# Fused linear attention and MLP on one core: batch 2's loads lose a wait, the first unit's transposes and exps are reordered, and the planner gets new offsets

## The chip, the cores and the metric

One core of one Trainium2 chip. The metric is the device time of one execution in microseconds (us): lower is better. The engines of the core are TensorE (PE, matrix products and transposes), VectorE (DVE), ScalarE (ACT), GpSimd (POOL) and SyncE (SP, which here only issues transfers). PE's weight loads have a row of their own in the profile (PEld).

## The reference

```python
def phi(x):
    proj = np.einsum('bhsd,df->bhsf', x, w_phi)
    proj = proj - np.max(np.abs(proj), axis=-1, keepdims=True)
    return np.concatenate([np.exp(proj), np.exp(-proj)], axis=-1)
q_p, k_p = (phi(q), phi(k))                       # 8 batches x 8 heads x 576 x 256
kv = np.einsum('bhsf,bhsd->bhfd', k_p, v)
z = np.sum(k_p, axis=2)
num = np.einsum('bhsf,bhfd->bhsd', q_p, kv)
den = np.einsum('bhsf,bhf->bhs', q_p, z)[..., None] + 1e-06
x = (num / den), heads side by side               # 8 x 576 x 512
...
mu = np.mean(x, axis=-1, keepdims=True)
var = np.mean((x - mu) ** 2, axis=-1, keepdims=True)
xn = (x - mu) / np.sqrt(var + 1e-06) * g_ln
ch = np.maximum(xn @ w_ch1, 0.0) @ w_ch2          # 512 -> 2048 -> 512
return (x + ch).astype(np.float32)
```

q, k and v are 8 x 8 x 576 x 64 in float32; the profile counts 36.77 MB read and 9.44 MB written.

## The kernel before, in words

**Units.** The attention is cut into 32 units of two heads each, eight to a pair of batches (NPAIR = 4, H = 8). In the first two pairs (STAGED = 2) units 0 to 3 are four pairs of heads of one batch and units 4 to 7 those of the next; in the last two pairs unit i is head i of both batches. So batch 0 is units 0 to 3, batch 1 units 4 to 7, **batch 2 units 8 to 11**, batch 3 units 12 to 15. The 576 rows of a head are 512 main rows and a tail of 64; the tails of two heads share one mixed tile.

**A unit's stages.** Its q, k and v are loaded (`load_main`, `load_tails`, both through `issue`, L544, nearly all on SP) into three rotating buffers for two units each (qk0 to qk2, v0 to v2; tails in qx and vx). Units 0 to 7 are transposed on PE (`a_trans`: main tiles L688, the mixed tile L696, with copies out of PSUM on DVE or ACT); later units are cast to bf16 (L754, L759 on DVE, L761 on ACT, L763 on POOL, into three buffers b16) and transposed by a DMA (L782). The products with w_phi go into PSUM (k and q L876 or L882, tails L891, mixed tile L804/L805). DVE takes the maxima (L944), ACT the exps: exp(+k) and exp(-k) L958, the tails' L1024, the mixed tile's L821/L826/L830, and the factors em (L949) and en (L963) from the maxima, with which POOL scales v (vv, L968, L973, L977). PE forms kv (L1050, L1056), the result is copied as KV (L1064 on DVE, L1066 on ACT), PE forms the numerator (L1120, L1128, L1134), and the quotient is put into x (L1164, L1172, L1183, L1189); the part that lies on the other half of the partitions goes by way of xs and is moved by a transfer on SP (`x_158<-xs_132`, L1081).

**The MLP.** A pair of batches that is through gets its statistics (L1317), is centred (L1337 on DVE, L1342, L1347) and transposed: the first pair on PE with copies that apply g (L1278, L1288 on DVE, L1290 on ACT), the others by DMA (L1303). Then follow the products with w_ch1 (L1396), the relu into hT_all (L1405 on DVE, L1407 on ACT), the products with w_ch2 (L1465), the result with the residual (L1473 on DVE, L1478 on ACT with L1484 on POOL), and the store. The weights are loaded in four parts each on POOL's queue, converted on the way: w_ch1 by `load_w1` (L636), each part once the unit named in GATE has come; w_ch2 by `load_w2` (L647).

**What sets the order.** Nothing is ordered by hand: each operation is entered into a planner (class `Order`, L153) with its engine or engines, an estimate of its duration, what it reads and writes and a rank. `run` (L204) plays the program through and gives each engine, whenever it comes free, the ready operation of the lowest rank; that order is what is emitted. An operation's rank is the latest time at which it may start for the rest to be in time, plus an offset from the table OFF, chosen by the unit (`stage_table`, L1536) and the stage. One number can so move many instructions. Each engine then runs its list strictly in order and waits where an operand is missing. Where the planner sees PE idle before WARM = 75 us, it puts a filler into PE's order (`fill`, L1676): a product of zeros, `wz`, of 120 columns.

**The hold.** A load that is entered with `hold=True` waits for the fourth part of w_ch2 (`wait_for_w2`, L559, HOLD = 3), on the chip as in the plan. In the kernel before these are the loads of units 8 to 15, that is of batches 2 and 3. The load stands in SP's order, so all that SP issues behind it waits too.

## Time and profile before

| what | value |
|---|---|
| runs | 376.31, 374.83, 377.27 us; median 376.31 |
| profiled execution | 375.71 us, of which 373.9 us in the span |
| granted clock of PE | 1.0 |
| products with w_ch1 (L1396) and w_ch2 (L1465) | 152.5 and 139.2 us of PE's time |
| DVE maxima (L944) | 77.2 us |
| ACT exps of k (L958) and of the tails (L1024) | 61.0 and 60.2 us |
| transfers | 53.39 MB, 143 GB/s in the mean |

The span is the time from the profile's first to its last instruction. Busy times of engines overlap; a group is named by its line, engine, operation and out<-in with buffer numbers left out. A row of the waits reads: the waiting engine and what it wanted to run, an arrow, what came last, then total, number and longest wait. The chain of work that ended last gives start, length and what ran. "SPq" is SP as the issuer of transfers, "DMA" the transfer itself.

### The profile page before, as it was taken

To read this page: it belongs to the slowest core of one execution; us is meant where nothing else is said; L and a number is where in the kernel's file an instruction comes from. 1 tells how busy PE (TensorE), PEld (TensorE's weight loads), DVE (VectorE), ACT (ScalarE), POOL (GpSimd) and SP (SyncE) were. 2 spreads that over 40 slices of the span, in tenths; PEclk is the share of its full clock that TensorE was granted. 3 is DMA by queue.
4 is the path that set the end of the run, shared out by engine and by line. 5 is a ranking of instruction groups with operands and counts; after the bars stand their busy time and mean duration, and the time that the engine had idled before them with its cause. 6 is when DMAs were issued, how large, how long until landed. Compare 5 with 4: busy or idle time off the path is not lost.

```text
span 373.9 us, 9770 instructions
## 1 busy us (share of the span) xinstructions
PE 361.6 (97%) x3732; PEld 229.5 (61%) x3776; DVE 246.3 (66%) x548; ACT 269.5 (72%) x586; POOL 203.6 (54%) x340
## 2 busy tenths in 40 slices
PE   8999999999899999999999999999999999999996
PEld 8889865556556655556566755655656555555544
DVE  4679998869779998988867899758786900000001
ACT  2888987786959996986978797787775845444430
POOL 4539757798575669956767608367456321011112
PEclk9999999999999999999999999999999999999999
DMA  8999979999997776686751539330000361010012
GB/s 205 285 236 268 193 204 253 224 244 234 300 191 186 209 180 203 145 219 127 233 136 33 132 100 168 93 65 29 31 30 30 86 127 46 12 56 28 31 56 84
DMA packets 91438, 53.39 MB, mean 143 GB/s; under 512 B 57840, under 2 KB 86832, under 8 KB 91392
## 3 DMA queue, kind: packets, MB, share of 16 engines
q1 hardware_dynamic: 86352, 47.73, 52.1%
q0 software_dynamic: 4416, 4.49, 7.3%
q10 hardware_dynamic: 624, 0.56, 0.6%
q8 instruction: 29, 0.48, 0.5%
q14 instruction: 17, 0.14, 0.1%
HBM read 36.77 MB, written 9.44 MB: 124 GB/s over the span
## 4 chain that ended last, share of the span: by engine, by line
PE 82%; DMA 5%; DVE 5%; ACT 4%; issue 1%; SPq 1%; POOL 0%; DVEq 0%; ACTq 0%
PE b_bank L1396 31%; PE b_bank L1465 30%; PE n_bank L1677 4%; PE a_bank L882 3%; PE n_bank L1056 3%; DMA qk<-in_q_dram 3%; PE a_bank L1128 2%; PE a_bank L891 2%; DVE m L944 2%; DMA qkT<-b 2%; PE n_bank L1050 1%; ACT ea L1024 1%; PE b_bank L1430 1%; PE n_bank L1128 1%; ACT eb L958 1%
## 5 line engine op out<-in xcount | busy, mean ns | idle before, releaser
L1396 PE MATMUL b_bank<-xT,w 128*128 128x384 bf16 (+2 forms) x768 | 152.5, 326 | 0.8 <-ACT hT_all L1407 0.3
L1465 PE MATMUL b_bank<-w,hT_all 128*128 128x512 bf16 x519 | 139.2, 379 | 2.0 <-issue 0.2
L1396 PEld LDWEIGHTS <-w 128*128 128x128 bf16 x768 | 70.9, 98 | 54.8 <-issue 2.2
L1407 ACT ACTIVATE hT_all<-b_bank 128x384 bf16<-128x384 f32 (+2 forms) x126 | 61.9, 492 | 53.8 <-PE b_bank L1396 53.0
L944 DVE TENSOR_REDUCE m<-a_bank 128x8 f32<-128x1024 f32 x64 | 77.2, 1215 | 16.3 <-PE a_bank L882 13.2
L1465 PEld LDWEIGHTS <-hT_all 128*128 128x128 bf16 x560 | 51.0, 98 | 42.3 <-issue 1.3
L1484 POOL TENSOR_TENSOR o<-o,x 128x512 f32<-128x512 f32 x22 | 25.4, 1156 | 70.6 <-ACT o L1478 65.5
L958 ACT ACTIVATE eb<-a_bank 128x1024 bf16<-128x1024 f32 x60 | 61.0, 1045 | 3.8 <-DVE m L944 3.7
L1024 ACT ACTIVATE ea<-a_bank 128x1024 bf16<-128x1024 f32 x60 | 60.2, 1040 | 2.7 <-PE a_bank L891 1.0
L968 POOL TENSOR_TENSOR vv<-v,em 128x512 bf16<-128x512 f32 x30 | 31.4, 1048 | 34.4 <-ACT em L949 23.2
L1172 POOL TENSOR_TENSOR x<-numc,rden 128x192 bf16<-128x192 f32 (+2 forms) x44 | 25.0, 572 | 38.2 <-DVE rden L1164 37.3
L1405 DVE TENSOR_SCALAR hT_all<-b_bank 128x384 bf16<-128x384 f32 (+2 forms) x66 | 36.7, 558 | 9.2 <-PE b_bank L1396 8.5
L1473 DVE SCALAR_TENSOR_TENSOR o<-b_bank,rstd,x 128x512 f32<-128x512 f32 x13 | 9.7, 744 | 47.3 <-issue 25.9
L968 POOL TENSOR_TENSOR vv<-v,en 128x512 bf16<-128x512 f32 x30 | 31.4, 1047 | 2.0 <-ACT en L963 1.9
L1677 PE MATMUL n_bank<-wz 128*128 128x120 bf16 x389 | 29.1, 228 | 0.0
L1128 PEld LDWEIGHTS <-ea 128*128 128x128 bf16 x448 | 22.0, 97 | 9.1 <-issue 2.1
L1677 PEld LDWEIGHTS <-wz 128*128 128x128 bf16 x411 | 25.9, 105 | 1.0 <-issue 0.3
L1056 PE MATMUL n_bank<-vv,eb 128*128 128x65 bf16 x480 | 25.2, 194 | 0.0
L1317 DVE BATCH_NORM_STATS2 st<-x 128x6 f32<-128x256 bf16 (+1 forms) x52 | 25.0, 506 | 0.1
L1056 PEld LDWEIGHTS <-eb 128*128 128x128 bf16 x480 | 20.9, 98 | 3.5
L1478 ACT ACTIVATE o<-b_bank,rstd 128x512 f32<-128x512 f32 x22 | 15.1, 686 | 10.0 <-PE b_bank L1465 9.7
L882 PE MATMUL a_bank<-wbk,qkT 64*128 64x128 bf16 x448 | 19.7, 217 | 0.3 <-DMA qkT<-b 0.3
(132 smaller groups left out, 509.4 us busy)
## 6 DMA issues: line engine op xcount, KB each, us to landing
out_dram<-o SPq DMA_DIRECT2D x31, 256.0 KB, 2.5
qk<-in_k_dram SPq DMA_DIRECT2D x24, 256.0 KB, 4.8
qk<-in_q_dram SPq DMA_DIRECT2D x23, 256.0 KB, 5.4
v<-in_v_dram SPq DMA_DIRECT2D x23, 256.0 KB, 4.3
w<-in_moe_w_ch_dram POOLq DMA_DIRECT2D x8, 512.0 KB, 11.8
qk<-in_k_dram SPq DMA_DIRECT2D x4, 512.0 KB, 5.5
qk<-in_q_dram SPq DMA_DIRECT2D x4, 512.0 KB, 6.9
v<-in_v_dram SPq DMA_DIRECT2D x4, 512.0 KB, 7.4
```

The costliest lines, as they stand in the source:

```text
L882: nc.tensor.matmul(ps[:, half * 4 + c, :], u["qkT"][rows, cols], wbk[rows, half, :], start=True, stop=True,)
L944: nc.vector.reduce_max(out=m, in_=ps, axis=AX.X, apply_absolute_value=True)
L958: nc.scalar.activation(eb, ps, AF.Exp, scale=(1.0, -1.0)[t])
L968: nc.gpsimd.tensor_tensor(out=u["vv"][:, t, 0:MX, 0:D], in0=vb[:, hh, :].rearrange("p (c d) -> p c d", d=D), in1=bcast(e[:, 0:MX], 2, D), ...
L1024: nc.scalar.activation(u["EA"][:, t, 0:1024], u["pt"], AF.Exp, scale=(1.0, -1.0)[t])
L1056: nc.tensor.matmul(ps[:, t, c // 4, :], EB[:, t, c, :], vv[:, t, c, :], start=False, stop=(t == 0 and c == MX - 1), skip_group_check=True,)
L1128: nc.tensor.matmul(ps[t][:, i, :], ea(u, t, c), KV[:, t, c // 4, :], start=True, stop=True,)
L1396: nc.tensor.matmul(st["ps"], w1_sb[:, kc, jj * P : (jj + 1) * P], xT_bufs[(pair * NR + r) % XB][:, kc : m * KC : KC, :], start=(kc == 0), ...
L1405: nc.vector.tensor_relu(h_sb, st["ps"])
L1407: nc.scalar.activation(h_sb, st["ps"], AF.Relu)
L1465: nc.tensor.matmul(ch[t], hT[r, jj][:, rt * P : (rt + 1) * P], w2_sb[:, jj, :], start=(jj == 0), stop=(jj == JC - 1),)
L1677: nc.tensor.matmul(banks[res][i][:, 0:WN] if res else warm, wz, wz[:, 0:WN], start=bool(res), stop=bool(res), skip_group_check=True,)
```

## The change

1. **The hold** is kept only for units 12 to 15 (batch 3). The loads of units 8 to 11, main rows and tails, no longer wait for w_ch2, in the plan or on the chip.
2. **The first unit's transposes**: k, q, then the mixed tile; before: k, mixed tile, q. The key "T", which tied the transposes to one another in the plan, is gone.
3. **exp(+k) of units 0 to 3** is no longer entered as waiting for the maximum of its k: exp(+k) doesn't use it; exp(-k) of the same unit still waits.
4. **Twelve offset tables instead of ten**, all with new numbers: units 8 to 11, 12 to 15, 16 to 23 and 24 to 31 now have a table each; before, units 8 to 15 shared one and units 16 to 31 another.
5. `res="B"` instead of `"A"` in the later pairs: the name of the PSUM bank for transposes on PE, which units 8 to 31 don't make.

```diff
 OFF = (
...
-        "load": 251.7, "trans": -68.1, "trans.copy": 96.2, "mixed": 136.9, "mixed.max": -693.9,
...
+        "load": 341.1, "trans": -218.6, "trans.copy": 96.2, "mixed": -294.3, "mixed.max": 64.5,
...
@@ -581,7 +597,7 @@
-                262144 * nu, hold=HOLD >= 0 and H <= n < 2 * H,
+                262144 * nu, hold=12 <= n < 2 * H,
@@ -592,7 +608,7 @@
-                [(key + str(half), g % NBUF, u) for u in us], 131072 * nu, hold=HOLD >= 0 and n < 2 * H,
+                [(key + str(half), g % NBUF, u) for u in us], 131072 * nu, hold=12 <= n < 2 * H,
@@ -612,7 +628,7 @@
-                row=4096 if queue == "POOL" else 256, hold=HOLD >= 0 and H <= n < 2 * H, n=n,
+                row=4096 if queue == "POOL" else 256, hold=12 <= n < 2 * H, n=n,
@@ -718,8 +734,7 @@
-            add("PE", mm(1, 128), rank, mixed, r=data, w=[("qxT_ps", n), ("T", j, 2), "T"],
-                acquire=("B", 1))
+            add("PE", mm(1, 128), rank, mixed, r=data, w=[("qxT_ps", n), ("T", j, 2)], acquire=("B", 1))
@@ -728,7 +743,7 @@
-                w=[("qkT_ps", n), *[("T", j, i) for i in which], "T"],
+                w=[("qkT_ps", n), *[("T", j, i) for i in which]],
@@ -740,8 +755,8 @@
             add_main((1,))
+            add_main((0,))
             add_mixed()
-            add_main((0,))
@@ -1004,7 +1019,7 @@
-        add("ACT", 0.92, rk("k.exp", n), lambda: exps(0), r=[ps_key, ("m", i, n % 4)],
+        add("ACT", 0.92, rk("k.exp", n), lambda: exps(0), r=[ps_key, *([("m", i, n % 4)] if n >= 4 else [])],
@@ -1534,7 +1549,7 @@
     def stage_table(n):
-        return min(n, H) + (n >= 2 * H)
+        return n if n < H else H + (n >= H + 4) + (n >= 2 * H) + (n >= 3 * H)
@@ -1559,7 +1574,7 @@
-                u.update(res="A", res1="N")
+                u.update(res="B", res1="N")
```

The shown rows of OFF are the first of units 8 to 15 before and of units 8 to 11 after; the other rows differ in the same manner. What the new numbers do is seen in the engines' orders. In these, line numbers of the changed kernel are 15 or 16 higher; sizes are partitions x elements, and x2 is two like instructions in a row.

The first place is SP's order behind the loads of unit 3. qk2 and v2 there take units 4 and 5, qk0 and v0 units 6 and 7 (with qk0 first used by units 0 and 1), v1 unit 3. Before:

```order
L544 DMA v1_97<-in_v_dram 128x2x256
L544 DMA v2_99<-in_v_dram 128x2x256 x2
L544 DMA qx1_83<-in_k_dram 64x4x64 x2
L544 DMA qx1_83<-in_q_dram 64x4x64 x2
L544 DMA qk2_98<-in_k_dram 128x2x256
L544 DMA qk2_98<-in_q_dram 128x2x256
L544 DMA qk2_98<-in_k_dram 128x2x256
L544 DMA qk2_98<-in_q_dram 128x2x256
```

With the change:

```order
L560 DMA v1_97<-in_v_dram 128x2x256
L560 DMA qk0_94<-in_k_dram 128x2x256 x2
L560 DMA qk0_94<-in_q_dram 128x2x256 x2
L560 DMA v2_99<-in_v_dram 128x2x256 x2
L560 DMA v0_95<-in_v_dram 128x2x256
L560 DMA qk2_98<-in_k_dram 128x2x256
L560 DMA qk2_98<-in_q_dram 128x2x256
```

The four loads of q and k of units 6 and 7 now stand ahead of those of units 4 and 5, together with a v of theirs, and the four tails of units 4 to 7 stand behind these rows.

The second place is SP's order at batch 2's loads: tails into qx0 and vx0, units 8 and 9 into qk1 and v1, units 10 and 11 into qk2 and v2. Before:

```order
L544 DMA v0_95<-in_v_dram 128x2x256 x2
L1081 DMA x_158<-xs_132 64x4x64
L544 DMA qx0_82<-in_k_dram 64x4x64 x2
L544 DMA qx0_82<-in_q_dram 64x4x64 x2
L544 DMA qk1_96<-in_k_dram 128x4x256
L544 DMA qk1_96<-in_q_dram 128x4x256
L544 DMA qk2_98<-in_k_dram 128x4x256
L544 DMA qk2_98<-in_q_dram 128x4x256
```

With the change:

```order
L560 DMA v0_95<-in_v_dram 128x2x256
L560 DMA qx0_82<-in_k_dram 64x4x64 x2
L560 DMA qx0_82<-in_q_dram 64x4x64 x2
L560 DMA qk1_96<-in_k_dram 128x4x256
L560 DMA qk1_96<-in_q_dram 128x4x256
L560 DMA vx0_100<-in_v_dram 64x4x64
L560 DMA qk2_98<-in_k_dram 128x4x256
L560 DMA qk2_98<-in_q_dram 128x4x256
L560 DMA vx0_100<-in_v_dram 64x4x64
L560 DMA v1_97<-in_v_dram 128x4x256
L1096 DMA x_158<-xs_132 64x4x64
L560 DMA v2_99<-in_v_dram 128x4x256
```

The move of batch 0's rows (x<-xs) stood ahead of all of batch 2's loads and now stands behind all of them but the last.

The third place is ACT's order around the cast of unit 16 (into b16_1). Before:

```order
L761 CAST b16_1_143<-qk2_98 128x1024
L949 ACTIVATE em_2020<-m2_113 128x12
L826 ACTIVATE eb0_147<-n_bank_152 128x128
L830 ACTIVATE ea0_121<-n_bank_152 128x2x64
L826 ACTIVATE eb0_147<-n_bank_152 128x128
L830 ACTIVATE ea0_121<-n_bank_152 128x2x64
L1290 ACTIVATE xT2_137<-b_bank2_157,ngln_80 128x2x128
```

With the change:

```order
L841 ACTIVATE eb0_147<-n_bank_152 128x128
L845 ACTIVATE ea0_121<-n_bank_152 128x2x64
L841 ACTIVATE eb0_147<-n_bank_152 128x128
L845 ACTIVATE ea0_121<-n_bank_152 128x2x64
L1305 ACTIVATE xT2_137<-b_bank2_157,ngln_80 128x2x128
L1305 ACTIVATE xT2_137<-b_bank0_155,ngln_80 128x2x128
L1305 ACTIVATE xT2_137<-b_bank1_156,ngln_80 128x2x128
```

That cast is no longer among ACT's instructions; it is now made on POOL (line 778 of the changed kernel), ahead of a vv product.

## The prediction

> **What bounds the kernel now.** I read the page first, then the busy time by stretch, then what TensorE (PE) waited for, and last the chain that ended last around its longest waits.

> ```profile
> span 373.9 us, 9770 instructions
> PE 361.6 (97%) x3732; PEld 229.5 (61%) x3776; DVE 246.3 (66%) x548; ACT 269.5 (72%) x586; POOL 203.6 (54%) x340
> L1677 PE MATMUL n_bank<-wz 128*128 128x120 bf16 x389 | 29.1, 228 | 0.0
> ```

> ```profile
> 0.00:10.00 10.00, 9.00 (x114) 8.96 (x115) 4.40 (x23) 2.98 (x4) 4.56 (x12) 1.00 0.86 212
> 10.00:75.00 65.00, 61.85 (x986) 49.40 (x987) 55.68 (x125) 54.31 (x111) 45.01 (x85) 1.00 1.10 237
> 75.00:120.00 45.00, 42.10 (x440) 26.05 (x447) 35.91 (x88) 36.50 (x85) 33.10 (x54) 1.00 1.00 231
> 120.00:290.00 170.00, 168.63 (x1767) 102.16 (x1792) 138.07 (x288) 138.15 (x314) 107.31 (x179) 1.00 0.49 121
> 290.00:374.00 84.00, 79.98 (x435) 42.95 (x439) 12.19 (x29) 37.53 (x75) 13.60 (x13) 1.00 0.22 59
> ```

> The columns of the second view are: stretch, its length, busy time of PE, of its weight loads, of DVE, ACT and POOL, granted clock, busy share of the DMA engines, GB/s. PE is busy for 168.6 of 170 us between 120 and 290 us, and the transfers fill all sixteen DMA engines (1.10 and 1.00) until 120 us. But PE's busy time up to 75 us is partly empty: L1677 is the filler, a product of zeros that the planner puts where it expects PE to have nothing. A filler stands in PE's order like work, so it costs its full time, and a wait of PE is never made good by dropping one. The span is therefore the real products, plus the fillers, plus PE's waits, plus the two ends. These are the waits of at least 0.3 us in the whole run (total, times, longest):

> ```profile
> PE b_bank L1278 <- ACT xT L1290: 1.3, 1, 1.3
> PE n_bank L1674 <- DVE wz L412: 1.0, 1, 1.0
> PE n_bank L1128 <- ACT KV L1066: 0.8, 1, 0.8
> PE b_bank L1128 <- DVE KV L1064: 0.8, 1, 0.8
> PE b_bank L1120 <- DVE x L1183: 0.6, 1, 0.6
> PE b_bank L1396 <- ACT hT_all L1407: 0.3, 1, 0.3
> PE a_bank L876 <- DVE m L944: 0.3, 1, 0.3
> PE a_bank L882 <- DMA qkT<-b: 0.3, 1, 0.3
> PE n_bank L804 <- ACT ea L830: 0.3, 1, 0.3
> ```

> They sum to 5.7 us, 4.7 without the one at the start, and all lie before 120 us. That, with the fillers, is all the change can win: the real products are the same.

> **Fillers.** The order of PE holds 412 products of wz before and 395 after: 17 fewer. Their price, from the chain in order of time (start, us, what):

> ```profile
> 1.28 3.90 PE n_bank L1677 x39
> 42.51 2.15 PE n_bank L1677 x41
> 156.80 1.73 PE b_bank L1396 x8
> ```

> 41 fillers took 2.15 us, 52 ns each, so 17 are worth 0.9 us. The first edits (q of the first unit transposed ahead of its mixed tile, the exp of +k free of the maximum, no "T" key) act in the first 45 us, where PE runs fillers: what they save can reach the end only as fewer fillers, so it is inside the 0.9. The other edits to code (the "B" for later pairs, which only units 0 to 7 would read; the map to the offset tables) issue nothing. The third row is for later: eight products of 512 columns in 1.73 us are 2.37 columns per ns.

> **The hold.** Batch 2's loads no longer wait for w_ch2. What SP, which issues all of these in order, waited for in the first 110 us, and the chain behind PE's wait at 60 us:

> ```profile
> SPq L1081 <- DVE xs L1189: 12.9, 1, 12.9
> ...
> SPq L544 <- DMA w<-in_moe_w_ch_dram: 2.2, 1, 2.2
> ```

> ```profile
> 51.29 6.53 DMA qk<-in_q_dram
> ...
> 57.95 1.18 DVE b L759
> ...
> 59.73 0.35 DVE KV L1064
> ```

> The hold itself cost SP 2.2 us. Ahead of it SP stood 12.9 us at the move x<-xs, from 32.1 to 45.0 us. The new order puts the move behind most of batch 2's loads, so both waits go for these, and units 8 and 9 can be loaded from some 33 us instead of 50.6. Before, their q landed at 57.8; DVE, in order, stood at its cast (L759), the KV copy came behind it, and PE waited 0.8 us for KV (L1128) and 0.3 us for the first DMA transpose (L882 <- DMA qkT). With the data 15 us earlier both should go: 1.1 us. Bounds 0 and 1.1; I take 1.1, since cast and load are parted by more than the 6.5 us that the load took.

> The lifted hold also puts 3 MB of loads beside w_ch2, which POOL now issues behind the vv products of units 2 and 3, partly behind unit 4's.

> ```profile
> L1465 PE MATMUL b_bank<-w,hT_all x519: 377/379/390, 75.0 to 366.5; 128*128 128x512 bf16 x173
> ```

> ```profile
> DMA to landing us min/median/max: 8.6/13.0/15.5
> ```

> The first product with w_ch2 is at 75.0. The second row is that of w_ch1, whose pieces moved among loads: 15.5 us at worst. POOL ended unit 4's vv at 40.4 before (L977), so w_ch2 is in by about 56: nothing.

> **The stretch from 75 to 120 us** holds the longest wait, 1.3 us, and another of 0.8:

> ```profile
> 87.52 5.44 DMA qk<-in_q_dram
> ...
> 93.06 1.04 ACT b L761
> ...
> 94.88 0.37 ACT xT L1290
> ...
> 99.48 6.88 DMA qkT<-b
> ...
> 107.41 0.37 ACT KV L1066
> ```

> ACT stood at the cast of unit 16 (L761) until its q had landed, and the xT copies for PE's L1278 were behind it. In the new order that cast is on POOL and no cast stands among ACT's xT copies. The second one came from a DMA transpose issued at 99.48: SP had 21 other transfers between the transposes of units 12 and 13 and those of 14 and 15, now 12. Bounds for the pair 0 and 2.1; both are at other work than the hold, and the casts wait elsewhere instead, so I take half: 1.05.

> **What the new order makes worse.** SP now loads q and k of units 6 and 7 (buffer qk0) ahead of unit 4's (qk2), and PE transposes unit 4 earlier. The columns ahead of that transpose on PE are 60.6 thousand before and 45.2 thousand now; 15.4 thousand at 2.37 per ns are 6.5 us.

> ```profile
> 31.44 0.61 PE L688 MATMUL b_bank<-ident,qk 128*128 128x128 bf16 x8
> ```

> ```profile
> L544 SPq DMA_DIRECT2D qk<-in_q_dram x2: 368/371/374, 17.2 to 19.4; - x2
> ...
> DMA to landing us min/median/max: 8.8/10.9/12.2
> ```

> ```profile
> 14.22 2.29 POOL L636 DMA_DIRECT2D w<-in_moe_w_ch_dram  x3
> 19.47 1.04 POOL L968 TENSOR_TENSOR vv<-v,em 128x512 bf16<-128x512 f32 x1 [2.96 <-ACT em L949]
> ```

> PE will ask for unit 4 at 31.4 - 6.5 = 24.9 us. Before, its q was issued at 17.2 and landed some 10 us later, at 27. Now five more loads of 256 KB stand ahead of it and four small ones fewer. Eight loads are in flight at once, so 10.9 us to land is 1.4 us per load: five of them put q at 34, less the small ones (0.5 each), 32. Against that, w_ch1 no longer moves from 14.2 us: its first piece stands behind the first vv of unit 1, that is at about 21. Without it loads of 4 to 10 us landed in 8.1 us, 1.0 per load:

> ```profile
> DMA to landing us min/median/max: 7.6/8.1/8.2
> ```

> Unit 3's v, issued at 9.0, lands at 17.1; unit 4's q is the ninth load after it: 26.1 at 1.0 per load, 29.4 at 1.36. So PE would wait 1.2 to 4.5 us; below nothing is excluded, but nothing is possible, as the last loads before w_ch1 may run faster than 1.0. I take 1.0, nearest to the free row, since w_ch1 starts at 21.

> **From 120 us on** PE waited for nothing before. In the new order kv of the last eight units stands 5 to 11 us earlier on PE, with DVE and ACT busy for 138 of 170 us. Bounds 0 and two waits like the longest, 2.6; I take 0, because of that slack. The other waits (0.6 and three of 0.3) I let recur: bounds -1.5 and 0.

> **The sum.** The profiled execution took 375.7 us, 1.8 around its span; the median of the runs is 376.3, 0.6 more. 375.7 - 0.9 - 1.1 - 1.05 + 1.0 = 373.65, and on the median 374.2: 0.6% faster. About 1%, 3.8 us, is what a measurement tells from no change.

> **Rivals.** *All waits go* (in full: -0.9 - 1.1 - 2.1 - 1.5, unit 4 in time): 370.1, on the median 370.7. For it: the three longest waits trace back to late transfers, and the transfers come earlier. Against: DVE and ACT are 84 to 86% busy from 10 to 75 us, so a new order only moves some waits. Chance 0.22. *The waits are swapped*: the hold cost 2.2 us of SP alone, the same number of waits comes back elsewhere, and only the fillers are won: 374.8, on the median 375.4. For it: PE has no slack, so each new wait counts. This is also the case in which lifting the hold does nothing by itself. Chance 0.22. *Unit 4 comes late*: w_ch1 starts before about 19 us, the loads of units 6 and 7 and unit 4's run at the shared pace, and PE waits the 4.5 us: 375.7 - 0.9 + 4.5 = 379.3, on the median 379.9, slower. It decides as soon as q lands after 26. For it: the rows above; against: the order of POOL. Chance 0.12. The forecast has 0.44.

> [...]

> **How the numbers follow.** Beside the forecast, both ends of the unknown costs lie in the range: 370.5 leaves out only the upper rival's last fifth of a microsecond and beyond, 378.0 holds forecast and swap with 2.6 us of late waits and leaves out the slower rival. Faster by over 1% (below 372.5): the first rival and a sixth of the forecast, 0.29. Slower by over 1% (over 380.1): half of the last rival and a little for late waits, 0.08. Within 1%: 0.63.

> **What would show it.** Right: 395 fillers; SP issues batch 2's first k at 31 to 36 us with no wait on w_ch; the waits L1128 <- DVE KV and L882 <- DMA qkT gone from PE's list; L1278 <- ACT xT below 0.5 us; L1465 beginning at 74 to 75 us; still no waits of PE after 120. Wrong: a wait of over 2 us at the transposes of L688 (now about L704) around 25 us, PE waits that sum to more than 6 us, or a first L1465 after 77 us.

## The result and the profile after

The changed kernel takes 371.5 us (371.29 to 372.2, 4 runs) where the kernel before takes 376.36 us (374.83 to 377.27, 4 runs beside it): a ratio of 0.9878, with a 95% interval of 0.9843 to 0.9913, so 1.2% faster. The forecast was 374.2, 0.6% faster; "all waits go" was 370.7. The measured time lies nearer to that rival, and the gain is about twice the forecast's.

The page of the kernel after, first the span, then busy times, then the filler's row (L1692 is L1677 of before):

```profile
span 369.6 us, 9733 instructions
PE 359.8 (97%) x3713; PEld 227.1 (61%) x3759; DVE 245.2 (66%) x559; ACT 265.9 (72%) x581; POOL 203.1 (55%) x334
...
L1692 PE MATMUL n_bank<-wz 128*128 128x120 bf16 x380 | 27.4, 224 | 0.1
```

The span is 4.3 us shorter: PE is busy 1.8 us less, nearly all of it in the fillers' row (29.1 us before), and idle 2.5 us less. Busy time by stretch, columns as in the prediction's view of the same kind:

```profile
0.00:10.00 10.00, 8.55 (x118) 8.07 (x119) 5.43 (x22) 4.55 (x6) 4.55 (x12) 1.00 0.86 206
10.00:75.00 65.00, 62.65 (x974) 49.20 (x979) 55.22 (x127) 56.77 (x120) 44.61 (x80) 1.00 1.11 250
75.00:120.00 45.00, 44.52 (x484) 27.68 (x490) 40.04 (x98) 38.60 (x89) 32.68 (x58) 1.00 0.96 231
120.00:290.00 170.00, 168.30 (x1738) 101.42 (x1759) 139.81 (x301) 133.26 (x302) 109.62 (x176) 1.00 0.49 117
290.00:369.60 79.60, 75.82 (x412) 40.73 (x417) 4.75 (x13) 32.74 (x67) 11.62 (x10) 1.00 0.21 60
```

Length less PE's busy time is its idle time. Between 75 and 120 us it was 45.00 - 42.10 = 2.90 us and is 0.48; between 10 and 75 us 3.15 and is 2.35; from 120 to 290 us 1.37 and is 1.70. (Those two are most likely gaps in the record: some 40 products with w_ch2 are missing in both traces, and where none is missing, as in the run below without 85 fillers, PE has no idle time there.) So most of the idle time that went, went between 75 and 120 us. What PE waited for in the whole run, all rows of that view of the kernel after:

```profile
PE n_bank L1689 <- DVE wz L428: 1.0, 1, 1.0
PE b_bank L1143 <- ACT KV L1081: 0.8, 1, 0.8
PE b_bank L1480 <- issue: 0.5, 3, 0.2
PE b_bank L819 <- ACT qkT L721: 0.4, 1, 0.4
PE a_bank L906 <- ACT hT_all L973: 0.4, 1, 0.4
PE b_bank L1143 <- DVE numc L1173: 0.2, 1, 0.2
```

Of the waits of before, the 1.3 us for the xT copy, both waits for KV at 60 and 108 us, the 0.6 us for x and the 0.3 us for the DMA transpose are gone. One of 0.8 us for KV is new, at 47 us.

How far PE is with its real products shows the place best. This table is summed from the PE records: columns of all products but the fillers, in units of 2400 columns, each about 1 us of PE's work at the prediction's 2.37 columns per ns (records are missing in each trace, so a difference of some tenths says nothing).

```
time, us          45     60     75     85     95    110    120    290
before         20.45  31.58  43.55  53.22  61.45  74.28  84.05 248.85
after          21.15  30.94  44.46  54.45  64.07  78.60  87.95 252.59
hold lifted    20.08  31.58  43.55  53.43  62.78  76.52  86.30 251.20
```

Up to 60 us the changed kernel has no lead. At 75 us the lead is 0.9, at 85 us 1.2 and at 110 us 4.3, of which 3.7 are left at 290 us. Between 60 and 75 us PE runs 12 fillers where it ran 30, and is idle for 0.27 us where it was 1.00: both go together, since real work is there earlier. The third row is the first experiment.

### The profile page after: what moved, and what is told of

The parts are those of the page before. It is cut to its first block, busy times and chain, and to the rows that moved or that the text cites. A ratio compares the mean times of both kernels' runs of the same rounds, so it can differ in the third digit from the quotient of the medians.

```text
span 369.6 us, 9733 instructions
## 1 busy us (share of the span) xinstructions
PE 359.8 (97%) x3713; PEld 227.1 (61%) x3759; DVE 245.2 (66%) x559; ACT 265.9 (72%) x581; POOL 203.1 (55%) x334
## 4 chain that ended last, share of the span: by engine, by line
PE 88%; DVE 5%; ACT 4%; issue 2%; DVEq 0%
PE b_bank L1411 34%; PE b_bank L1480 31%; PE n_bank L1071 4%; PE a_bank L897 4%; DVE m L959 3%; PE n_bank L1692 3%; PE a_bank L1143 2%; PE a_bank L906 2%; PE n_bank L1065 1%; PE b_bank L1445 1%; PE n_bank L1143 1%; ACT eb L973 1%; PE n_bank L1149 1%; PE a_bank L881 1%; PE n_bank L819 1%
## 5 line engine op out<-in xcount | busy, mean ns | idle before, releaser
L1422 ACT ACTIVATE hT_all<-b_bank 128x384 bf16<-128x384 f32 (+2 forms) x122 | 60.4, 495 | 55.3 <-PE b_bank L1411 54.8
L1420 DVE TENSOR_SCALAR hT_all<-b_bank 128x384 bf16<-128x384 f32 (+2 forms) x70 | 38.4, 549 | 8.7 <-PE b_bank L1411 8.0
L983 POOL TENSOR_TENSOR vv<-v,en 128x512 bf16<-128x512 f32 x30 | 32.3, 1078 | 2.5 <-issue 2.0
L1692 PE MATMUL n_bank<-wz 128*128 128x120 bf16 x380 | 27.4, 224 | 0.1
L1692 PEld LDWEIGHTS <-wz 128*128 128x128 bf16 x394 | 24.0, 102 | 1.2 <-issue 0.5
L1264 POOL TENSOR_TENSOR x<-numc,rden 128x384 bf16<-128x384 f32 (+1 forms) x24 | 15.1, 638 | 12.8 <-DVE rden L1179 12.6
## 6 DMA issues: line engine op xcount, KB each, us to landing
w<-in_moe_w_ch_dram POOLq DMA_DIRECT2D x8, 512.0 KB, 10.9
```

The lines of the kernel that those rows point to most:

```text
L983: nc.gpsimd.tensor_tensor(out=u["vv"][:, t, 0:MX, 0:D], in0=vb[:, hh, :].rearrange("p (c d) -> p c d", d=D), in1=bcast(e[:, 0:MX], 2, D), ...
L1420: nc.vector.tensor_relu(h_sb, st["ps"])
L1422: nc.scalar.activation(h_sb, st["ps"], AF.Relu)
L1692: nc.tensor.matmul(banks[res][i][:, 0:WN] if res else warm, wz, wz[:, 0:WN], start=bool(res), stop=bool(res), skip_group_check=True,)
```

## The experiments

Except in the two runs marked as planned anew, the orders of all engines are kept instruction by instruction: the planner's finished order is taken, and single entries in it are moved or dropped. `shift` puts the entries with the first numbers behind the one with the last; `fills` are the fillers that reach PE's order.

**The hold alone.** The plan is the old one; only the wait on the chip goes.

```diff
-            if hold:
+            if hold and n >= 12:
                 wait_for_w2(load)
```

> The kernel before with every engine's order kept; only the wait on w_ch2 of the loads of units 8 to 11 is taken away on the chip. Theory A (late transfers are the cause, but the hold is not what made them late: SP stood 12.9 us at the move x<-xs ahead of it): SP's 2.2 us go, q of unit 8 lands at about 55.6 instead of 57.8, PE's wait of 0.8 us at L1128 <- DMA KV shrinks, 376.4 becomes 375.6 to 376.2. Theory B (the hold itself is the gain): both waits around 60 and 68 us go and later loads follow, 375.3 or less. Theory C (the gain is in the order of copies on ACT and POOL): no change, 376.4 within 0.4.

373.35 us (372.05 to 375.33, 12 runs), ratio 0.994 (0.9912 to 0.9967): 2.3 us, half of the whole gain, and more than theory A gave it. But the 0.8 us at 60 us stay, and the wait at 95 us is gone. Three of PE's waits in this kernel:

```profile
PE b_bank L696 <- DMA qx<-in_q_dram: 1.2, 1, 1.2
...
PE b_bank L1128 <- DVE KV L1064: 0.8, 1, 0.8
...
PE n_bank L1128 <- ACT KV L1066: 0.3, 1, 0.3
```

The first, at 9.5 us, stands ahead of all that the edit touches and is not in the trace of before. It costs nothing: by 60 us PE is as far as in the kernel before (31.58 in the table). Up to there something other than PE sets the pace.

ACT at the cast of unit 16 in the kernel before, where it stood idle for 2.0 us, then in this kernel:

```profile
93.06 1.04 ACT L761 CAST b<-qk 128x1024 bf16<-128x1024 f32 x1 [2.02 <-DMA qk<-in_q_dram]
```

```profile
90.13 1.04 ACT L761 CAST b<-qk 128x1024 bf16<-128x1024 f32 x1
...
91.95 0.50 ACT L1290 ACTIVATE xT<-b_bank,ngln 128x256 bf16<-128x256 bf16 x1
```

The cast finds its q landed and starts without a wait, 2.9 us earlier, so the xT copies behind it are in time for PE. The 2.2 us that SP stood at the hold at 45.7 us had travelled down its queue, past batches 2 and 3, to the loads of batch 4: unit 16's last q is issued at 84.8 instead of 87.5. On the way SP is ahead of the kernel before by 2.0 us at the first tails, 1.4 at the first transpose, 2.2 at the fourth and 2.95 at the tails issued just ahead of unit 16's loads. So the wait was paid some 45 us behind its place. This trace is of an execution of 373.18 us; five of the twelve took 374.7 us or more, and whether the wait is back in those isn't shown. PE's busy time in the stretch where it was paid, 85 to 112 us, of the kernel before, with the hold lifted, and of the changed kernel:

```profile
85.00:112.00 27.00, 24.31 (x253) 15.06 (x253) 21.29 (x48) 20.41 (x44) 19.25 (x35) 1.00 1.04 244
```

```profile
85.00:112.00 27.00, 26.26 (x271) 16.40 (x277) 22.83 (x51) 22.87 (x54) 21.31 (x38) 1.00 1.00 255
```

```profile
85.00:112.00 27.00, 26.68 (x269) 16.21 (x269) 22.82 (x53) 22.32 (x55) 20.43 (x34) 1.00 0.90 250
```

2.69 us idle, then 0.74, then 0.32: of the 2.37 us of idle time that the changed kernel loses there, the lifted hold takes away 1.95 alone.

**The loads ahead of the move x<-xs as well**: the tails of q, k and v of batch 2, q and k of units 8 to 11, and v of units 8 and 9.

```diff
-            if hold:
+            if hold and n >= 12:
...
+    shift(done, (239, 241, 243, 245, 251, 253, 247, 345, 347, 249, 255), 166)
```

> As the run without the hold, and eleven loads of batch 2 stand ahead of the move x<-xs in SP's order; every other engine's order is that of the kernel before. Theory A: SP issues unit 8's q at 31 to 36 us, the waits L1128 <- DVE KV (0.8) and L882 <- DMA qkT (0.3) go, and what stands behind on SP comes earlier too, so that the waits at 95 and 108 us (1.3 and 0.8) shrink: 373.2 to 375.3. If the move to x now comes too late for the first MLP, PE waits before 60 us instead: 377 or more. Theory C: within 0.4 of 376.4, since DVE's, ACT's and POOL's orders are the old ones.

373.44 us (12 runs), ratio 0.9945 (0.9925 to 0.9965): no more than the lifted hold alone. Unit 8's q was issued at 37.8 us, 13.5 earlier than before, and landed at 55.1, 2.7 earlier. Between 10 and 75 us the transfers keep all sixteen DMA engines busy (a share of 1.14 here): this load took 17.3 us to land instead of 6.5, beside w_ch2 and the last part of w_ch1, which landed between 40.7 and 56.6 us. And the waits at 60 us and, in the profiled execution (374.9 us, one of the longer of the twelve, with unit 16's last q issued at 86.3), at 95 us are there:

```profile
PE b_bank L1278 <- ACT xT L1290: 1.2, 1, 1.2
...
PE b_bank L1128 <- DVE KV L1064: 0.8, 1, 0.8
```

Why did the earlier data not help at 60 us? DVE's cast of unit 8 in the kernel before, then in the kernel with the hold lifted, and behind each what POOL did there:

```profile
57.95 1.18 DVE L759 CAST b<-qk 128x1024 bf16<-128x1024 f32 x1 [0.92 <-DMA qk<-in_q_dram]
```

```profile
57.76 0.82 POOL L1249 TENSOR_TENSOR x<-numc,rden 128x384 bf16<-128x384 f32 x1
```

```profile
57.19 2.12 DVE L759 CAST b<-qk 128x1024 bf16<-128x1024 f32 x1
```

```profile
57.22 0.75 POOL L763 TENSOR_TENSOR b<-qx,one 128x128 bf16<-128x128 f32 x2
57.94 0.82 POOL L1249 TENSOR_TENSOR x<-numc,rden 128x384 bf16<-128x384 f32 x1
```

The cast no longer waits 0.92 us for q, but takes 2.12 us instead of 1.18 and ends at the same time, 59.3 against 59.1. The shortest casts of this size on DVE take 0.68 us (two in the changed kernel, at 73 and 92 us). Both casts here end 0.55 us after POOL's product with rden (59.13 after 58.58, 59.31 after 58.76), and so does the cast of the next experiment (58.71 after 58.16). POOL works beside the short casts as well (its product with rden, begun 0.07 us after the cast at 73.01, takes 1.30 us instead of 0.82), so what makes the cast longer here is not shown.

**The cast behind the KV copy.** With the hold lifted, DVE's cast of unit 8 is put behind the relu and the KV copy.

```diff
+    shift(done, (404,), 402)
```

> The kernel before with the hold of units 8 to 11 lifted on the chip, and DVE's cast of unit 8 (L759) put behind the relu and the KV copy (L1064) that followed it. Theory P (the cast, 2.1 us beside POOL's work, is what PE waited for at 60 us, not the late q): the wait of 0.8 us at L1128 <- DVE KV goes, and 372.6 to 373.0 if nothing takes its place. Rival (unit 8's transpose, now up to 3 us later, brings a wait of its own behind 68 us): 373.4 or more.

373.88 us (12 runs), ratio 0.9954 (0.9933 to 0.9976), against 0.994 with the hold lifted alone. The wait at 60 us is gone from PE's list, so the cast was its cause; but two later ones are longer, 0.7 instead of 0.3 us and 0.4 where there was none, and nothing is won. The time is the rival's. Its reason, a wait for unit 8's transpose behind 68 us, is not seen: the two waits are those at 108 and 95 us, and how the moved cast brings them stays open.

```profile
PE n_bank L1128 <- ACT KV L1066: 0.7, 1, 0.7
...
PE b_bank L1278 <- ACT xT L1290: 0.4, 1, 0.4
```

**ACT's cast of unit 16 moved** (the kernel before otherwise, hold included).

```diff
+    shift(done, (903,), 747)
```

> The kernel before, with one instruction moved: ACT's cast of unit 16 (L761) stands 11 instructions later, behind the xT copy, two exps of the tails and en. Theory C (the order on ACT): PE's wait of 1.3 us at L1278 <- ACT xT goes and nothing takes its place: 375.1. Theory A: ACT has 2.0 us less to wait at 93 us, but the transpose of unit 16 and what is behind it on SP is as late as before, so the wait returns in part elsewhere: 375.7 to 376.4.

375.18 us beside 375.77 (12 and 35 runs), ratio 0.9994 (0.9966 to 1.0022). The wait of 1.3 us is no longer in PE's list, yet the gain is not told from none. The 1.3 us of theory C lie at the very edge of the interval; theory A's 0 to 0.7 fits.

**Fewer fillers in the kernel before.** In the end 10 fillers went, not 17: 7 of the planner's last 17 entries never reach PE's order, since no bank is free for them at that time.

```diff
+    for o in [o for o in done if o.number < 0][-17:]:
+        done.remove(o)
```

> The kernel before without the last 17 of its 412 fillers (all after 60 us), every other instruction in its place. Theory A, as in the forecast (a filler costs its time like work): 17 x 52 ns = 0.9 us less, 375.5. Rival (fillers stand where PE would have waited anyway): PE's waits between 60 and 75 us grow by what the fillers took, 376.4 within 0.3.

375.78 beside 375.77 us, ratio 1.0008 (0.9985 to 1.0031). The 0.9 us of theory A lie outside; the 0.5 us that ten fillers come to lie at the edge. The waits do not settle it either: for KV at 108 us PE waited 1.4 us where it was 0.8, but for the xT copy 0.7 where it was 1.3, and its idle time from 60 to 112 us is 3.83 us where it was 3.80:

```profile
PE n_bank L1128 <- ACT KV L1066: 1.4, 1, 1.4
...
PE b_bank L1278 <- ACT xT L1290: 0.7, 1, 0.7
```

Ten fillers are too few to be told from the spread of the executions (374.83 to 377.31).

**Fewer fillers where the later waits are gone.** The same question with more of them: the hold lifted, and the last 85 fillers that do reach PE's order left out (327 stay).

```diff
+    for o in fills[-85:]:
+        done.remove(o)
```

> The kernel before with the hold of units 8 to 11 lifted on the chip, and without the last 85 of its 412 fillers (those after 45 us). Theory A, as in the forecast (a filler costs its time): 85 x 52 ns = 4.4 us less than the run that only lifted the hold (373.4): 369. Rival (fillers fill what PE waits for anyway, DVE, ACT and the transfers set the pace to 112 us): 373.4 within 0.7, with PE's waits up by some 4 us. Third case: PE's waits get long enough for the clock to fall: over 374.

372.14 us (6 runs), ratio 0.9901 (0.9874 to 0.9928), against 0.994: about 1.4 us, with intervals that overlap, where 4.4 us would be a ratio of 0.982. So a filler here costs roughly a third of its time. The rest PE waited: from 45 to 75 us it is idle for 3.9 us, where with the hold lifted alone it was 1.5.

**Fewer fillers in the changed kernel**, the last 75 (320 stay), and, in another run, every third one behind the first 100 (296 stay, never two left out in a row).

```diff
+    for o in fills[-75:]:
+        done.remove(o)
```

```diff
+    for o in fills[71::3]:
+        done.remove(o)
```

> The changed kernel without the last 75 of its 395 fillers (those after 45 us). Theory A: 75 x 52 ns = 3.9 us less than 371.5: 367.6. Rival (they stand where PE would wait): 371.5 within 0.7. Third case: the clock falls in the longer waits: over 372.5.

> The changed kernel without every third filler behind the first 100 (98 of 395 dropped, from 10 us on, at most one in a row). Theory A (a filler costs its time): 98 x 52 ns = 5.1 us less, 366.4. From the run without the last 85 in the kernel before (1.2 of 4.4 us came back): a quarter, 1.3 us less, 370.2. If PE is so little busy that the clock falls, as in the run without the last 75 (half rate from about 50 to 57 us, 1.8 us slower): over 372.5.

The first took 373.26 us (6 runs), ratio 0.9939 (0.9916 to 0.9962): slower than the changed kernel by 0.6%, or 2.3 us by the ratios. PE had no wait over 1.2 us, but was busy for less than half of the time from 46 to 50 us, and the granted clock (the column ahead of the DMA share) fell:

```profile
46.00:48.00 2.00, 0.87 (x26) 0.73 (x21) 2.00 (x4) 1.85 (x7) 0.95 (x1) 1.00 1.19 235
48.00:50.00 2.00, 0.95 (x16) 0.64 (x15) 2.00 (x4) 1.19 (x6) 0.31 (x1) 1.00 1.17 245
50.00:52.00 2.00, 0.96 (x8) 0.79 (x8) 2.00 (x4) 1.59 (x4) 0.51 (x1) 0.54 1.17 246
...
56.00:57.00 1.00, 1.00 (x12) 0.71 (x11) 0.74 (x2) 1.00 (x2) 1.00 (x1) 0.52 1.14 321
57.00:58.00 1.00, 1.00 (x6) 0.48 (x5) 0.51 (x3) 1.00 (x2) 0.91 (x2) 1.00 1.12 332
```

The thinned one took 370.35 us (370.25 to 370.96, 4 runs), ratio 0.9868 (0.9845 to 0.9892), with the clock at 0.999. That is the best time of all, but its ratio is not told from the changed kernel's 0.9878. 99 fillers of 52 ns (395 less 296 in the traces), 5.1 us, were worth 0.4 us by the ratios; 5.1 is far outside the intervals. So the fillers do two things: they cost little, because they stand where PE has little to do, and without the last 75 of them the granted clock fell to 0.50 from 50.1 to 57.0 us, where thinned they were enough for 0.999 in the mean.

**The hold in the new order.** The changed kernel, with batch 2's loads behind the move and waiting for w_ch2 again.

```diff
-            if hold:
+            if hold or n == 8 or n == 10:
                 wait_for_w2(load)
...
+    shift(done, (239, 241, 243, 245, 251, 253, 247, 345, 347, 249, 255), 285)
```

> The changed kernel with every order kept but SP's: the eleven loads of batch 2 stand behind the move x<-xs again, and all of batch 2's loads wait for the fourth part of w_ch2 again. Theory H (the hold costs its 2.2 us in any order, as in the run that only lifted it): w_ch2 lands at about 50 us without these loads beside it, unit 8's q at 57 to 60 instead of 50.4, the transposes of units 8 to 10 some us later; PE waits 2 to 4 us between 60 and 112 us: 373.5 to 375.5. Theory O (the new order has the casts where ACT and DVE do not stand in front of others, so late loads cost nothing): 371.5 within 0.5.

379.43 us (6 runs), ratio 1.0102 (1.0074 to 1.0131): 7.9 us more than the changed kernel, over theory H. Unit 8's q landed at 62.2, and ACT stood for it with everything that PE needed behind the cast; the timeline of ACT, then PE's wait and the stretches around it:

```profile
62.31 1.04 ACT L776 CAST b<-qk 128x1024 bf16<-128x1024 f32 x1 [5.74 <-DMA qk<-in_q_dram]
...
65.08 0.60 ACT L1422 ACTIVATE hT_all<-b_bank 128x512 bf16<-128x512 f32 x1
```

```profile
PE b_bank L1143 <- ACT hT_all L1422: 4.9, 1, 4.9
```

```profile
60.00:66.00 6.00, 1.12 (x10) 0.56 (x9) 2.10 (x6) 3.69 (x5) 2.14 (x2) 0.77 1.12 309
66.00:72.00 6.00, 6.00 (x50) 2.90 (x47) 1.95 (x3) 4.02 (x7) 5.03 (x11) 0.67 1.16 259
```

PE waited 4.9 us in one piece, and then ran at half clock until 70 us: 0.33 x 6 = 2.0 us more, an estimate from the 0.67 granted from 66 to 72 us. That is 6.9 of the 8.8 us by which this trace's span is longer than the changed kernel's. The new order needs the early loads; it is not that late loads cost it nothing.

**The tables alone, and the code alone.** Both orders are planned anew.

The first is the kernel before with this, the whole of OFF included; the second the changed kernel with the same taken back.

```diff
 OFF = (
...
-        "load": 251.7, "trans": -68.1, "trans.copy": 96.2, "mixed": 136.9, "mixed.max": -693.9,
+        "load": 341.1, "trans": -218.6, "trans.copy": 96.2, "mixed": -294.3, "mixed.max": 64.5,
...
-        return min(n, H) + (n >= 2 * H)
+        return n if n < H else H + (n >= H + 4) + (n >= 2 * H) + (n >= 3 * H)
```

> The kernel before with the twelve new offset tables and the new map to them alone; the hold for units 8 to 15, the first unit's order and the wait of exp(+k) are the old ones, and the planner makes its order anew. If the tables carry the half that the lifted hold does not explain (4.7 us in all, 2.3 by the hold): 374. If they only fit the lifted hold: 376 or more, with new waits of PE around 60 us, since the plan has SP stand at w_ch2.

> The changed kernel's code (hold for units 12 to 15 alone, q ahead of the mixed tile, exp(+k) free of the maximum) with the old ten tables and the old map; the order is planned anew. If the hold's 2.2 us come through whatever the order: 373 to 374.3. If the other edits save the fillers' 0.9 us as the forecast had it, up to 372.5. If the old tables do not fit the new plan: 376 or more.

The tables alone take 401.25 us (4 runs), ratio 1.068 (1.0645 to 1.0715); the code alone 385.3 us (four executions from 384.51 to 386.2), ratio 1.0257 (1.0223 to 1.0291). Neither part is an improvement by itself. With the tables alone PE's waits come mostly between 230 and 254 us, some 15 us of them, the last and longest of 7.5 us, and the clock falls there. That is not the place that was expected, 60 us, and why this order goes wrong so late stays open:

```profile
PE n_bank L1066 <- DVE mv L1349: 7.5, 1, 7.5
```

```profile
225.00:235.00 10.00, 5.66 (x78) 3.45 (x76) 5.01 (x11) 8.81 (x19) 8.32 (x14) 0.87 0.51 113
235.00:250.00 15.00, 7.93 (x113) 5.84 (x110) 12.19 (x29) 9.38 (x19) 10.03 (x17) 0.61 0.51 103
```

**w_ch1 early in the new order**, the forecast's slower rival brought about.

```diff
+    shift(done, (145, 148, 151), 87)
```

> The changed kernel with one move on POOL: the first three parts of w_ch1 are issued behind unit 0's vv, at about 14.8 us, as in the kernel before, instead of 22.0 and 25 us. The forecast's rival (unit 4 comes late): loads land 1.36 us apart instead of 0.75, unit 4's q at 27 to 28.5 instead of 24.03, and PE, which asks for it at 24.06, waits 3 to 4.5 us at L704: 374.5 to 376. If what PE loses there is made good later, because DVE and ACT set the pace from 25 to 75 us: 371.5 to 373.

378.89 us (6 runs), ratio 1.0108 (1.0064 to 1.0151): 7.4 us over the changed kernel. The loads of q and k of units 4 and 5 (issued between 16 and 20 us) in the changed kernel, then here, and PE at unit 4's transposes here:

```profile
DMA to landing us min/median/max: 6.2/6.5/7.0
```

```profile
DMA to landing us min/median/max: 10.4/12.5/14.6
```

```profile
27.18 0.61 PE L704 MATMUL b_bank<-ident,qk 128*128 128x128 bf16 x4 [2.14 <-DMA qk<-in_k_dram]
29.31 0.61 PE L704 MATMUL b_bank<-ident,qk 128*128 128x128 bf16 x4 [1.52 <-DMA qk<-in_q_dram]
```

```profile
27.00:28.00 1.00, 0.61 (x4) 0.35 (x4) 0.00 (x0) 0.53 (x1) 0.00 (x0) 0.60 1.16 247
28.00:29.00 1.00, 0.00 (x0) 0.00 (x0) 0.00 (x0) 0.00 (x0) 0.00 (x0) 0.50 1.19 245
...
33.00:34.00 1.00, 1.00 (x10) 0.81 (x8) 0.96 (x3) 0.46 (x1) 0.00 (x0) 0.50 1.22 204
34.00:35.00 1.00, 1.00 (x18) 0.98 (x17) 0.82 (x2) 1.00 (x3) 0.25 (x1) 0.98 1.22 224
```

PE waits 3.7 us, inside the 3 to 4.5 expected, and the clock stands at half from 27.2 to 34.0 us; PE is busy at that rate for 5.3 us, half of which, by estimate, is the price: some 2.6 more. In the profiled execution, 377.1 us and the shortest of the six, the span is 5.7 us longer than that of the changed kernel, so these two, 6.3 us, cover all of it. What the longer executions lose beyond that, no profile here shows.

## Why the prediction was right, and where not

The sign, the size within its range and the places where it said the order would show (395 fillers; batch 2's first k issued at 29.8 us, a little ahead of the 31 to 36, with no wait on w_ch; L1128 <- DVE KV, L882 <- DMA qkT and L1278 <- ACT xT gone; the first product with w_ch2 at 74.0; no wait after 120 us) came true. The sum was 2.05 us of span, the chip's 4.3. By its terms:

- **Fillers, 0.9 us.** The step "a filler stands in PE's order like work, so it costs its full time, and a wait of PE is never made good by dropping one" failed. Ten fewer gave nothing that can be seen, 85 fewer roughly a third of their time, 99 fewer a tenth of it. Most of what the 85 had taken, PE then waited: it was idle for 3.9 us instead of 1.5 between 45 and 75 us. At a third, the 17 of this change are worth 0.3 us.
- **The hold, 1.1 us at 60 to 68 us.** The sum was too small and the place wrong. Lifted alone, the hold is worth 2.3 us, nearly all of it between 85 and 112 us, where the prediction said of the waits that "both are at other work than the hold". It followed SP's delay to the next loads only, and not down the queue to unit 16's q, for which it had quoted the row itself. The remark in the rival of swapped waits that lifting the hold may do nothing by itself is refuted.
- **"With the data 15 us earlier both should go."** Issued 19 us earlier, q landed only 7.4 us earlier (50.4 against 57.8) in the changed kernel, and 2.7 us earlier in the experiment, as the DMA engines were full (shares of 1.11 and 1.14 from 10 to 75 us). Nor did the wait at 60 us follow the data: the cast took 2.12 us instead of 1.18 and ended no earlier (59.3 against 59.1), 0.55 us behind POOL's product. The new order got rid of that wait by other means: ACT and POOL make unit 8's casts there (from 55.0 us), and DVE has none of that size ahead of its KV copy.
- **75 to 120 us, half of 2.1.** This is the term that was mis-sized: idle time fell from 2.90 to 0.48 us, 2.4, more than the whole of both waits. The casts' order was not needed for the first wait (with the hold lifted it goes though the cast stands where it stood).
- **Unit 4, 1.0 us.** It was not late, but only just: q landed at 24.03, PE began unit 4's transposes with k at 24.06 and came to q at 24.29. PE's request was forecast at 24.9. Without w_ch1, loads landed 0.75 us apart up to 21.4 us, below the 1.0 that was taken as the free pace. That the mechanism was real is shown by the run with w_ch1 early, which gives the rival's place and wait; that its time, 378.89 us, is close to the 379.9 forecast for it is luck, since the rival had a wait of 4.5 us and no lower clock, and left out the gains elsewhere.
- **After 120 us, 0**: right, no wait of over 0.2 us.

By place, the three terms up to 75 us come to 0.9 + 1.1 - 1.0 = 1.0 us, and the table has a lead of 0.9 there, though none of the three came as forecast: that is luck. The difference between sum and span, 2.3 us, lies mostly between 75 and 120 us, where 1.05 was forecast and the lead grows by 3.0 us (2.4 by idle time). How the remaining 2.4 us of gain, beside the hold's 2.3, divide among the new order's parts stays open: table and code cannot be run apart without a new plan, and the two runs that did so are slower for waits of their own. The share of the first unit's edits was not tried by itself.

## What to carry to other kernels

A wait in an in-order queue of transfers can be paid far behind its place, where an item of the queue comes too late, here some 45 us on (SP's 2.2 us at 45.7 us were 1.95 us of PE's idle time between 85 and 112 us): look down the queue past the work next to it. Issuing a load earlier need not move its data as far: with the DMA engines full, 13.5 us of earlier issue were worth 2.7 us here, and 19 us were worth 7.4. An order that is planned as a whole fits the waits that it was planned with: half of such a change can cost more than the whole gains.

## What the runs showed of the hardware

```profile
28.25:31.66 3.41, 1.12 (x25) 0.95 (x23) 0.42 (x2) 3.32 (x4) 3.41 (x7) 1.00 1.01 158
31.66:35.07 3.41, 3.41 (x41) 3.10 (x37) 2.57 (x10) 1.11 (x2) 0.21 (x1) 0.50 1.14 198
35.07:38.48 3.41, 3.41 (x75) 3.40 (x73) 2.75 (x6) 2.14 (x9) 0.51 (x1) 1.00 1.13 230
```

In the step of 3.41 us that ended with the fall, PE was busy for 0.31 of the time with the hold in the new order, for 0.33 in the first row here and for 0.37 with w_ch1 early; without 75 fillers it was busy for 1.82 of the 4 us from 46 to 50. In the kernels before and after, steps of 0.62 (at 92 us) and 0.71 (at 45 us) were not followed by a fall. The returns in those four runs came at the end of a step in which PE was busy throughout, and steps of 0.56 (w_ch1 early) and about 0.7 (without 75 fillers) brought none. PE was not idle for the whole of any of the steps ahead of these falls: with w_ch1 early the clock fell 2.2 us after PE had run dry, and without 75 fillers it fell with no wait over 1.2 us. What sets the clock beyond that is not shown.

With w_ch1 early the wait of 3.7 us fell into two steps, busy for 0.37 and 0.56: the clock fell at the end of the first and was still at half in the step behind the second. That cost some 2.6 us by the estimate made at that run.
